# Attention and MLP on one core: the order of q and x transposes in SP's queue

## The chip, the cores and the metric

The kernel runs on one core of one Trainium2 chip. The metric is device time in microseconds for one execution. Five engines run side by side, each with a queue of its own: TensorE (PE in the profile, its weight loads PEld), VectorE (DVE), ScalarE (ACT), GpSimd (POOL) and SyncE (SP). SP computes nothing here; it issues DMAs.

## The reference

Four sequences of 768 positions, 8 heads of 64. Attention sees four sink positions and a window of 128; the result goes through a layer norm and a two-layer MLP with a residual:

```python
keep = is_sink | in_window            # 4 sinks, 0 <= rel < 128
scores = np.where(keep, scale * q @ k.T, -1e9)
a = softmax(scores)
x = (a @ v) as (B, S, 512)
xn = (x - mu) / sqrt(var + 1e-6) * g_ln
out = x + relu(xn @ w_ch1) @ w_ch2    # 512 -> 2048 -> 512
```

## The kernel before, in words

The rows are cut into 24 tiles `t` of 128 rows, and into 12 chunks `c` of two tiles. Six tiles make a sequence. For each chunk the kernel loads k, q and v, transposes k and q (`kT`, `qT`), and computes scores, exponentials, masks and the product with v for each tile. `normalise` then takes mean and variance of the result `x`, writes the centred tile `xc` (L866) and transposes it into `xnt`. `mlp(c)` reads `xnt` of both tiles of its chunk: first layer (L1027, 64 matmuls for a chunk), relu on ScalarE (L1037), second layer (L1056), and the sum with the residual `ot` (L1064), which SP stores (L1068).

Where transposes are done changes along the way. k and q of chunks below `by_dma` = 4, and x of chunks below `x_by_dma` = 3, are transposed by TensorE and copied out of PSUM. From there on they are DMA transposes that SP issues, all from one line, L571 (`dma_t`), told apart by their tiles: `kT<-nat`, `qT<-nat` and `xnt<-xc`, two of each for a chunk.

The work of tiles from the fourth chunk on is in `block(t)`: on TensorE it holds the product with v of tile t-1 (L934, L941, L950) and the scores of tile t (L961, and L969 for the sinks on even t). So tile 7 gets its product with v, and with it `xc`, in block 8; and q of chunk c is first read by block 2c. The MLP of chunk c-2 runs between block 2c-1 and block 2c: `xnt` of tile 2c-3 must be there by then. Second-layer matmuls (L1056) of older chunks fill the time between blocks.

The order on every engine is made by a planner written out in the kernel. Each piece of work is a `P.op` with a name, the engines that it may run on, a priority, its buffers and its predecessors. `Plan.run` walks through them with estimated durations, including estimates of when a DMA lands, and gives each engine a fixed order; the program is then emitted in that order. A predecessor given with `after=` counts for these estimates, and so for the order. What the engines wait for on the chip comes from the buffers that the emitted instructions read and write.

Loads of k, q and v are issued by GpSimd (L671 for k and q, L595 for v). `gate(c)` holds the loads of a chunk in the planner behind the GpSimd part of the layer norm of an earlier tile (`rs_op`, L871 and L872): for c > 5 that of tile 2c-4, for c = 5 that of tile 5. On SP, each k transpose then follows its load, and so does each q transpose; the x transpose follows `xc`, and the store follows `ot`. At the start of a sequence SP also issues two small copies `vs_s<-vs` (L540).

Of the kernel before, what the change touches and what calls it, by code (L numbers as in the profile page):

```python
# [196 lines left out]
def pe(us):  # L197
    return {"PE": (us, us + Plan.PE_DRAIN)}
# [12 lines left out]
def fix(occ, extra=0.09):  # L211
# [8 lines left out]
HW_X = (1.0, -0.2, 0.6)  # L220
# [10 lines left out]
PAR = dict(strict=400.0, win=0.4, tr=-8.0, sc=-5.0, sc1=-2.0, av=2.0, blk=-8.0, step=6.0, trx=9.0, by_dma=4, x_by_dma=3,  # L231
           w1p=(1.6, 2.6, 2.7, 2.8), pm=3, w2p=(4.5, 4.51, 4.52, 4.53), apart=2, vs0=(2.0, 13.0), by_tile=1, vp=(0.0, 0.1, 2.0, 2.1, 4.55, 4.56), ld1=0.05)
# [135 lines left out]
def kernel(  # L368
# [32 lines left out]
    P = Plan()  # L401
# [104 lines left out]
    def negs(e):  # L506
# [17 lines left out]
         writes=[Bc["gt"]], dma=HW_T)  # L524
    for h in range(H):
# [3 lines left out]
            reads=[Bc["vc"]], writes=[Bc["vcd"]], nb=3.5 + 0.55 * h)  # L529
    for b in range(B):  # L530
# [4 lines left out]
            reads=[Bc["vcd"], Bc["vc"], Bc["sel4" if b else "sel"]], writes=[Bvs[b]], nb=PAR["vs0"][1] if b == 0 else 40.0 * b)  # L535
# [11 lines left out]
    for c in range(4):  # L547
        P.op(f"w2ld{c}", {"POOL": (0.75, 0.8)}, PAR["w2p"][c], lambda e, c=c: G.dma_start(
            w2[c], moe_w_ch2[512 * c:512 * (c + 1), :].rearrange("(t p) n -> p t n", p=128)),
            writes=[Bw2[c]], dma=SW_W)  # L550

    def at(c, step):
        return 16.0 * c - 8.0 + PAR[step]
# [3 lines left out]
    xnt_b = [Buf(f"xnt{c}", "xnt") for c in range(NC)]  # L557
# [4 lines left out]
    def early(t):  # L562
        return 0.5 + 0.8 * t

    rs_op = {}

    def gate(c):
        return [rs_op[2 * c - (4 if c > 5 else 5)]] if PAR["by_dma"] < c < NC else []

    def dma_t(dst, src):  # L570
        nc.sync.dma_start_transpose(out=dst, in_=src)  # L571
# [26 lines left out]
    def evict(name, prio, n, src, dst, reads, writes, fp=False):  # L598
        du = {"ACT": act(n), "DVE": dve(n) if fp else dve(n, 0.52)}
        P.op(name, du, prio, lambda e: (nc.scalar.copy if e == "ACT" else V.tensor_copy)(dst(), src()),  # L600
             reads=reads, writes=writes)

    def chunk(c):
        b, R = c // RC, c % RC
        d = at(c, "tr") if c >= 2 else early(2 * c)
        ld = d - 14.0 if c >= RC else 4.0
        if c < 2:
            kT_b[c], qT_b[c] = Buf(f"kT{c}", "kT"), Buf(f"qT{c}", "qT")
            if c == 0:
                nats = [Buf("kf", "natf"), Buf("qf", "natf")]  # L610
                for hh in range(2):
                    hs = slice(4 * hh, 4 * hh + 4)
                    for i, (x, T) in enumerate(((k, kT_b[c]), (q, qT_b[c]))):
                        nm, src, part = "kq"[i], nats[i], Buf(f"{'kq'[i]}l{hh}")
# [4 lines left out]
                        nat, pt, done = Buf(f"{nm}c{hh}", "natc"), Buf(f"pt{nm}{hh}", "one"), Buf(f"{nm}T0{hh}")  # L619
                        P.op(f"cast{nm}{hh}", {"DVE": dve(512), "ACT": act(512)}, d + 0.01 * hh,  # L620
                             lambda e, nat=nat, src=src, hs=hs: (nc.scalar.copy if e == "ACT" else V.tensor_copy)(
                                 nat.t, src.t[:, hs].rearrange("p h i d -> p i h d")),
                             reads=[part], hold=[src], writes=[nat])

                        def tr(e, pt=pt, nat=nat):
                            pb = pt.t.rearrange("p (h m i) -> p h m i", h=2, i=2)
                            for hp in range(2):
                                for i in range(2):
                                    nc.tensor.matmul(pb[:, hp, :, i], lhsT=nat.t[:, i, 2 * hp:2 * hp + 2, :], rhs=ident,  # L629
                                                     start=hp + i == 0, stop=True, skip_group_check=True)  # L630
# [7 lines left out]
            for t in (2 * c, 2 * c + 1) if c else ():  # L638
                d, at_t = early(t), slice(128 * (t % 2), 128 * (t % 2) + 128)
                if c:  # L640
                    pt = Buf(f"pt{t}", "one")
                    for i, (x, T) in enumerate(((k, kT_b[c]), (q, qT_b[c]))):
                        nat = Buf(f"{'kq'[i]}n{t}", "nat")
                        ap = x[b, :, 128 * t:128 * t + 128, :].rearrange("h p d -> p h d")
                        P.op(f"{'kq'[i]}ld{t}", {"POOL": (0.87, 0.9)}, PAR["ld1"] + 0.2 * (t - 2) + 0.01 * i,
                             lambda e, nat=nat, ap=ap: G.dma_start(nat.t, ap), writes=[nat], dma=SW)

                        def tr(e, nat=nat, pt=pt, i=i):
                            pb = pt.t.bitcast(BF16)
                            for hp in range(HP):  # L650
# [3 lines left out]
                                       reads=[nat, Bc["ident"]], hold=[T], **({"rw": [pt]} if i else {"writes": [pt]}))]  # L654
# [6 lines left out]
        else:  # L661
            for nm, src, bT in (("k", k, kT_b), ("q", q, qT_b)):
                T = Buf(f"{nm}T{c}", nm + "T")
                bT[c] = T
                pt = Buf(f"pt{nm}{c}", "one")
                for i in range(2):
                    if c >= PAR["by_dma"]:
                        nat = Buf(f"{nm}n{c}{i}", "nat")
                        ap = src[b, :, 256 * R + 128 * i:256 * R + 128 * (i + 1), :].rearrange("h p d -> p h d")
                        P.op(f"{nm}ld{c}{i}", {"POOL": (0.87, 0.9)}, ld + 0.01 * i + (0.1 if nm == "q" else 0.0),  # L670
                             lambda e, nat=nat, ap=ap: G.dma_start(nat.t, ap), writes=[nat], dma=SW, after=gate(c))  # L671
                        P.op(f"tr{nm}{c}{i}", {"SP": (1.2, 1.2)}, d + 0.01 * i, lambda e, T=T, nat=nat, i=i: dma_t(
                            T.t[:, :, 128 * i:128 * i + 128], nat.t.rearrange("p h d -> p (h d)")),
                            reads=[nat], writes=[T], dma=HW_X)
                        continue
                    nat = Buf(f"{nm}n{c}{i}", "nat")
                    ap = src[b, :, 256 * R + 128 * i:256 * R + 128 * (i + 1), :].rearrange("h p d -> p h d")
                    P.op(f"{nm}ld{c}{i}", {"POOL": (0.87, 0.9)}, ld + 0.01 * i + (0.1 if nm == "q" else 0.0),
                         lambda e, nat=nat, ap=ap: G.dma_start(nat.t, ap), writes=[nat], dma=SW)

                    def tr(e, nat=nat, pt=pt, i=i):
                        pb = pt.t.bitcast(BF16)
                        for hp in range(HP):
                            nc.tensor.transpose(pb[:, 256 * hp + 128 * i:256 * hp + 128 * (i + 1)],
                                                nat.t[:, 2 * hp:2 * hp + 2, :], ident)
                    P.op(f"tr{nm}{c}{i}", pe(0.224), d + 0.01 * i, tr, reads=[nat, Bc["ident"]], hold=[T],
                         **({"rw": [pt]} if i else {"writes": [pt]}))
                if c < PAR["by_dma"]:
                    evict(f"ev{nm}{c}", d + 0.2, 1024,
                      lambda pt=pt: pt.t.bitcast(BF16).rearrange("p (h c) -> p h c", h=HP),  # L690
                      lambda T=T: T.t, [pt], [T])
# [167 lines left out]
    def normalise(c, i, d, st, x, xc):  # L859
        t = 2 * c + i  # L860
        mv = Buf(f"mv{t}")
        P.op(f"bn{t}", {"DVE": fix(0.60)}, d + 0.12, lambda e: V.bn_stats(st.t[:, 8:14], x.t),  # L862
             reads=[x], writes=[st, mv])
        P.op(f"ag{t}", {"DVE": fix(0.09)}, d + 0.13, lambda e: V.bn_aggr(st.t[:, 14:16], st.t[:, 8:14]),  # L864
             reads=[st], rw=[mv])
        P.op(f"xc{t}", {"DVE": fix(0.26)}, d + 0.14, lambda e: V.tensor_scalar(  # L866
            xc.t, x.t, st.t[:, 14:15], None, op0=ALU.subtract), reads=[x, st, mv], writes=[xc])
        rs = Buf(f"rs{t}")
        xst_b[t, "rs"] = rs
        rs_op[t] = P.op(f"rs{t}", {"POOL": (0.83, 0.88)}, d + 5, lambda e: (  # L870
            G.tensor_scalar(st.t[:, 17:18], st.t[:, 15:16], 1e-6, None, op0=ALU.add),  # L871
            G.tensor_tensor(st.t[:, 16:17], st.t[:, 17:18], mhalf, op=ALU.pow)),  # L872
            reads=[st, mv, Bc["mhalf"]], writes=[rs])
        pt = Buf(f"ptx{t}", "one")

        def tr(e):
            pb = pt.t.bitcast(BF16)
            for j in range(NDM):
                nc.tensor.transpose(pb[:, 128 * j:128 * (j + 1)], xc.t[:, 128 * j:128 * (j + 1)], ident)  # L879
        if c >= PAR["x_by_dma"]:  # L880
            P.op(f"trx{t}", {"SP": (1.2, 1.2)}, d + 0.5, lambda e: dma_t(xnt_b[c].t[:, :, 128 * i:128 * i + 128], xc.t),
                 reads=[xc], writes=[xnt_b[c]], dma=HW_X)
            return
        d = at(c, "trx") + 1.0 * i if c >= 2 else d + 0.2
        P.op(f"trx{t}", pe(0.224), d, tr, reads=[xc, Bc["ident"]], writes=[pt],
             hold=[xnt_b[c]])
        src = lambda: pt.t.bitcast(BF16)[:, 0:512].rearrange("p (j c) -> p j c", j=NDM)
        dst = lambda: xnt_b[c].t[:, :, 128 * i:128 * i + 128]
        P.op(f"evx{t}", {"DVE": dve(512), "ACT": (1.2, 1.3)}, d + 0.1, lambda e: (
            V.tensor_tensor(dst(), src(), gt.unsqueeze(2).to_broadcast([128, NDM, 128]), op=ALU.mult) if e == "DVE" else  # L890
            [nc.scalar.mul(dst()[:, j], src()[:, j], gt[:, j:j + 1]) for j in range(NDM)]),
            reads=[pt, Bc["gt"]], writes=[xnt_b[c], xnt_t[t]])
# [191 lines left out]
    for c in range(NC):  # L1084
        mlp(c)
        if c == PAR["x_by_dma"] - 1:
            for s in range(4):
                for j in range(NDM):
                    P.op(f"w1g{s}{j}", {"DVE": fix(0.26)}, 16.0 * c + 11.0 + 2 * s + 0.1 * j,
                         lambda e, s=s, j=j: V.tensor_scalar_mul(w1[s][:, j, :], w1[s][:, j, :], gt[:, j:j + 1]),  # L1090
                         reads=[Bw1[s], Bc["gt"]], writes=[Bw1g[s]], after=last_use[s])

    def guard(e):
# [8 lines left out]
         reads=[pt_f], writes=[fl_b])  # L1102
# [4 lines left out]
    t = 1.2  # L1107
    for o in order:
# [5 lines left out]
        if n > 0 and o.start - t > 0.6:  # L1114
            free = [(max([e_ for b_, e_ in banks[i].lives if b_ < t], default=0.0), i) for i in range(8)
                    if all(e_ < t or b_ > o.start + 0.3 for b_, e_ in banks[i].lives)]
            if free:
                i = min(free)[1]
                items.append((t + 0.001, -n, pairs[i // 2][:, i % 2, :] if i < 4 else ones[i - 4]))
        t = o.start + o.engs["PE"][0]  # L1120
# [49 lines left out]
```

## Time and profile before

| | |
|---|---|
| median of 3 runs | 220.84 us (219.8 to 221.86) |
| profiled execution | 220.41 us |
| its span, first to last instruction | 218.8 us |
| TensorE busy | 208.0 us, 95% |
| VectorE, GpSimd, ScalarE busy | 118.3, 116.7, 105.3 us |
| granted TensorE clock | 1.000 |
| first layer L1027, second layer L1056 | 79.3 us and 84.8 us of TensorE |
| DMA transposes on SP | 16 of kT, 16 of qT, 18 of xnt, about 1.2 us each to issue |

Busy time is the time in which an instruction of the engine ran. A wait is idle time of an engine, put down to what ended it. On SP, a line of the timeline is the time that the queue took to issue a DMA (where two are merged, with the wait between them), not the time of the transfer. The transfer's end shows only where an instruction waited for it.

### The profile page before, as it was taken

The numbers are of one execution on the slowest core, as the hardware profiler recorded it, in microseconds if no ns is written. First come the engines' busy times: TensorE is split into PE (matmuls) and PEld (weight loads), VectorE is DVE, ScalarE is ACT, GpSimd is POOL, SyncE is SP. The second block draws the span as 40 slices with busy tenths as digits, with TensorE's granted clock in tenths as the row PEclk, the third lists the DMA queues.
The fourth block names the chain that finished last, engine by engine and source line by source line (L and its number), as shares of the span: only waits on it lengthen the run. The fifth ranks groups of instructions, "written<-read, shape, count | busy, mean of one in ns | idle before, by whom it ended". The sixth has DMA issues, their size and how long they took to land.

```text
span 218.8 us, 6430 instructions
## 1 busy us (share of the span) xinstructions
PE 208.0 (95%) x2630; PEld 146.1 (67%) x2653; DVE 118.3 (54%) x324; ACT 105.3 (48%) x167; POOL 116.7 (53%) x172
## 2 busy tenths in 40 slices
PE   6989999999999799999999999999999999999993
PEld 2658885774875585784775775774875875865852
DVE  5389882786996416716625626536445445444011
ACT  3668486254562371671571671671572562530610
POOL 7988582589972872592682692782871201201000
PEclk9999999999999999999999999999999999999999
DMA  5999999999999799299599399499699202202103
GB/s 154 162 182 206 175 206 198 158 150 120 205 146 168 126 149 140 49 170 118 122 159 179 58 163 132 113 148 144 117 137 154 90 3 75 72 3 72 48 9 105
DMA packets 110229, 27.81 MB, mean 127 GB/s; under 512 B 100464, under 2 KB 107248, under 8 KB 110192
## 3 DMA queue, kind: packets, MB, share of 16 engines
q0 software_dynamic: 76112, 13.18, 88.6%
q1 hardware_dynamic: 33024, 13.61, 33.3%
q10 hardware_dynamic: 1056, 0.52, 0.9%
q8 instruction: 23, 0.38, 0.8%
q14 instruction: 14, 0.11, 0.2%
HBM read 27.43 MB, written 6.29 MB: 154 GB/s over the span
## 4 chain that ended last, share of the span: by engine, by line
PE 87%; DVE 6%; DMA 2%; issue 2%; ACT 1%; SPq 0%; DVEq 0%
PE one L1056 36%; PE one L1027 35%; PE pair L961 3%; DMA xnt<-xc 2%; PE one L934 2%; PE pair L1126 2%; PE one L941 2%; DVE st L862 1%; DVE x L854 1%; PE one L950 1%; DVE xnt L890 1%; PE one L969 1%; PE pair L734 1%; PE one L629 1%; PE one L1020 1%
## 5 line engine op out<-in xcount | busy, mean ns | idle before, releaser
L1056 PE MATMUL one<-w,h 128*128 128x512 bf16 (+1 forms) x377 | 84.8, 370 | 2.2 <-issue 1.4
L1027 PE MATMUL one<-xnt,w 128*128 128x256 bf16 x704 | 79.3, 273 | 1.6 <-DMA xnt<-xc 1.6
L1037 ACT ACTIVATE h<-one 128x512 bf16<-128x512 f32 x95 | 56.6, 598 | 49.7 <-PE one L1027 46.4
L1027 PEld LDWEIGHTS <-w 128*128 128x128 bf16 x704 | 68.6, 98 | 12.4 <-DMA xnt<-xc 2.0
L1056 PEld LDWEIGHTS <-h 128*128 128x128 bf16 x400 | 37.3, 98 | 39.3
L979 ACT ACTIVATE pe<-pair 128x768 bf16<-128x768 f32 x36 | 27.2, 808 | 43.6 <-PE pair L961 39.2
L871 POOL TENSOR_SCALAR st<-st 128x1 f32<-128x1 f32 x24 | 8.7, 362 | 66.3 <-DVE st L864 65.7
L595 POOL DMA_DIRECT2D vn<-in_v_dram x59 | 38.7, 696 | 7.7 <-DMA w<-in_moe_w_ch_dram 3.3
L1002 DVE RECIPROCAL rec<-one 128x4 f32<-128x4 f32 x36 | 6.4, 177 | 59.6 <-PE one L950 48.1
L1064 DVE SCALAR_TENSOR_TENSOR ot<-one,st,x 128x512 f32<-128x512 f32 (+1 forms) x25 | 18.2, 728 | 13.1 <-PE one L1056 8.6
L872 POOL TENSOR_TENSOR st<-st,mhalf 128x1 f32<-128x1 f32 x24 | 16.6, 691 | 2.0
L862 DVE BATCH_NORM_STATS2 st<-x 128x6 f32<-128x512 bf16 x24 | 16.7, 695 | 0.8
L1004 DVE TENSOR_TENSOR x<-one,rec 128x256 bf16<-128x256 f32 x36 | 15.3, 425 | 1.2
L671 POOL DMA_DIRECT2D nat<-in_k_dram x16 | 15.1, 947 | 0.4 <-PE one L879 0.4
L671 POOL DMA_DIRECT2D nat<-in_q_dram x16 | 14.1, 897 | 0.0
L984 DVE TENSOR_TENSOR pe<-pe,band 128x768 bf16<-128x768 bf16 x24 | 12.3, 552 | 0.0
L866 DVE TENSOR_SCALAR xc<-x,st 128x512 bf16<-128x512 bf16 x24 | 8.8, 365 | 1.1 <-DVE st L864 0.3
L961 PE MATMUL pair<-qT,kT 64*64 64x128 bf16 (+1 forms) x528 | 9.2, 204 | 0.0
L759 ACT ACTIVATE pe<-pair 128x1024 bf16<-128x1024 f32 (+1 forms) x8 | 7.3, 920 | 3.6 <-PE pair L713 2.1
L934 PEld LDWEIGHTS <-pe 128*128 128x128 bf16 (+1 forms) x144 | 6.2, 97 | 2.9 <-issue 1.3
L1020 PE MATMUL one<-xnt,w 128*128 128x128 bf16 x128 | 7.8, 219 | 0.0
L961 PEld LDWEIGHTS <-kT 64*64 64x64 bf16 x528 | 7.2, 108 | 0.4 <-issue 0.4
(109 smaller groups left out, 171.8 us busy)
## 6 DMA issues: line engine op xcount, KB each, us to landing
out_dram<-ot SPq DMA_DIRECT2D x23, 256.0 KB
w<-in_moe_w_ch_dram POOLq DMA_DIRECT2D x8, 512.0 KB, 12.2
nat<-in_k_dram POOLq DMA_DIRECT2D x22, 128.0 KB, 4.9
nat<-in_q_dram POOLq DMA_DIRECT2D x22, 128.0 KB, 5.2
vn<-in_v_dram POOLq DMA_DIRECT2D x44, 32.0 KB, 5.2
vn<-in_v_dram POOLq DMA_DIRECT2D x15, 64.0 KB, 4.8
vn<-in_v_dram POOLq DMA_DIRECT2D x6, 128.0 KB, 6.5
natf<-in_q_dram ACTq DMA_DIRECT2D x2, 256.0 KB
```

The lines of the kernel that those rows point to most:

```text
L595: P.op(f"vld{t}_{i}", {"POOL": (0.8, 0.85)}, prio + 0.001 * i, lambda e, p0=p0, n=n, hs=hs, src=src: G.dma_start(m.t[p0:p0 + n, hs, 0:64], ...
L671: lambda e, nat=nat, ap=ap: G.dma_start(nat.t, ap), writes=[nat], dma=SW, after=gate(c))
L862: P.op(f"bn{t}", {"DVE": fix(0.60)}, d + 0.12, lambda e: V.bn_stats(st.t[:, 8:14], x.t), reads=[x], writes=[st, mv])
L872: G.tensor_tensor(st.t[:, 16:17], st.t[:, 17:18], mhalf, op=ALU.pow)),
L961: nc.tensor.matmul(pps[u].t[64 * g:64 * g + 64, h2, col + c0:col + c0 + n], lhsT=kt.t[rs, hp, k0:k0 + 64], rhs=qT.t[rs, hp, q0:q0 + n], st ...
L979: nc.scalar.activation(pes[j].t.rearrange("p a b -> p (a b)")[:, 0:768].rearrange("p (a b) -> p a b", a=2), pps[j].t[:, :, 0:384], AF.Exp, ...
L984: V.tensor_mul(at_s, at_s, band[j] if r > 1 else edge[r][j].unsqueeze(1).to_broadcast([128, 4, 192]))
L1004: P.op(f"x{t - 1}{u}", {"DVE": dve(256)}, d + 0.051 + 0.002 * u, lambda e, u=u, rc=rc, pv=pv: V.tensor_tensor(x.t[:, 256 * u:256 * u + 256 ...
L1027: nc.tensor.matmul(ph.t[:, 256 * s:256 * s + 256], lhsT=w1[ht // 4][:, j, 128 * (ht % 4):128 * (ht % 4 + 1)], rhs=xnt.t[:, j, :], start=j ...
L1037: nc.scalar.activation(hb.t, ph.t, AF.Relu)
L1056: nc.tensor.matmul(pc.t[:, 0:wd], lhsT=(h1[2 * s + i].t[:, 128 * ii:128 * ii + 128] if by_tile else h1[ht // 2].t[:, 256 * (ht % 2) + 128 ...
L1064: V.scalar_tensor_tensor(ot.t[:, sl], in0=pc.t[:, 0:wd], scalar=st.t[:, 16:17], in1=x.t[:, sl], op0=ALU.mult, op1=ALU.add),
```

## The change

For chunks c > 4, each of the two q transposes gets the x transpose of tile 2c-3 as a predecessor in the planner. That tile is three in front of the chunk's first tile, 2c. To have it at hand, `normalise` keeps the op of each x transpose in `trx_op`. No instruction is added or taken away, and k transposes, loads and stores keep their predecessors.

```diff
-    rs_op = {}
+    rs_op, trx_op = {}, {}
...
                         P.op(f"tr{nm}{c}{i}", {"SP": (1.2, 1.2)}, d + 0.01 * i, lambda e, T=T, nat=nat, i=i: dma_t(
                             T.t[:, :, 128 * i:128 * i + 128], nat.t.rearrange("p h d -> p (h d)")),
-                            reads=[nat], writes=[T], dma=HW_X)
+                            reads=[nat], writes=[T], dma=HW_X, after=[trx_op[2 * c - 3]] if c > PAR["by_dma"] and nm == "q" else [])
...
-            P.op(f"trx{t}", {"SP": (1.2, 1.2)}, d + 0.5, lambda e: dma_t(xnt_b[c].t[:, :, 128 * i:128 * i + 128], xc.t),
+            trx_op[t] = P.op(f"trx{t}", {"SP": (1.2, 1.2)}, d + 0.5, lambda e: dma_t(xnt_b[c].t[:, :, 128 * i:128 * i + 128], xc.t),
                  reads=[xc], writes=[xnt_b[c]], dma=HW_X)
```

## The prediction

> **What bounds the kernel now.** I read the page first: busy times, the chain that ended last, then the waits, the timeline of SP, and the stretches around each x transpose.
>
> The page says that TensorE carries the time. The first two lines are busy time, share of the span and instructions; the last is the chain by engine.
>
> ```profile
> span 218.8 us, 6430 instructions
> PE 208.0 (95%) x2630; PEld 146.1 (67%) x2653; DVE 118.3 (54%) x324; ACT 105.3 (48%) x167; POOL 116.7 (53%) x172
> ...
> PE 87%; DVE 6%; DMA 2%; issue 2%; ACT 1%; SPq 0%; DVEq 0%
> ```
>
> So a change on SP, which computes nothing, is worth only what TensorE waits for SP's transfers: look at the 2% of DMA. The waits of TensorE alone (us in total, times, longest) name it: one wait for a transposed x.
>
> ```profile
> PE pair L1126 <- DVE one_e L464: 1.8, 1, 1.8
> PE one L1027 <- DMA xnt<-xc: 1.6, 1, 1.6
> PE one L1056 <- issue: 1.4, 9, 0.2
> ```
>
> The first of these is in the startup, the third is nine gaps of at most 0.2 us that name no transfer. The middle one is the only place after the startup where TensorE stands. By stretches (length, then busy us and count of each engine) it lies in the stretch that ends at 73.2 us; afterwards every chunk looks alike:
>
> ```profile
> 63.00:73.20 10.20, 8.44 (x131) 4.33 (x121) 8.09 (x23) 3.32 (x6) 4.27 (x9) 1.00 1.61 128
> 73.20:89.60 16.40, 16.19 (x224) 11.55 (x227) 7.04 (x20) 8.09 (x13) 8.86 (x13) 1.00 1.76 135
> 89.60:105.50 15.90, 15.69 (x196) 10.77 (x196) 7.99 (x21) 7.97 (x13) 9.78 (x14) 1.00 1.72 134
> ...
> 154.00:170.20 16.20, 15.99 (x224) 11.33 (x225) 7.96 (x20) 8.08 (x13) 9.52 (x14) 1.00 1.47 133
> ```
>
> From 73.2 us on a chunk leaves TensorE 16.40 - 16.19 = 0.21 us idle (15.90 - 15.69 and 16.20 - 15.99 are the same 0.21), and none of that names a DMA. The granted clock is 1.00 in each of these stretches, so no clock is in play.
>
> **The one wait, step by step.** The timeline of that place, SP and VectorE and TensorE together (start, length, engine, operation, count, idle before):
>
> ```profile
> 59.60 5.61 SPq L571 DMA_TRANSPOSE kT<-nat  x2
> ...
> 65.38 2.72 SPq L571 DMA_TRANSPOSE qT<-nat  x2
> ...
> 65.69 0.35 DVE L866 TENSOR_SCALAR xc<-x,st 128x512 bf16<-128x512 bf16 x1
> ...
> 68.20 1.21 SPq L571 DMA_TRANSPOSE xnt<-xc  x1
> ...
> 69.97 1.67 PE L1056 MATMUL one<-w,h 128*128 128x512 bf16 x7 [0.16 <-issue]
> ...
> 73.19 3.01 PE L1027 MATMUL one<-xnt,w 128*128 128x256 bf16 x26 [1.55 <-DMA xnt<-xc]
> ```
>
> The centred tile 7 (`xc`) is ready at 65.69 + 0.35 = 66.04. SP has issued both k transposes of chunk 5 by 59.60 + 5.61 = 65.21, but then issues both q transposes (2.72 us), and only at 68.20 the x transpose of tile 7. TensorE has finished its other work at 69.97 + 1.67 = 71.64, and starts the MLP of chunk 3 at 73.19: 1.55 us idle. The chain of waits shows the transfer as 4.95 us from its issue:
>
> ```profile
> 67.14 0.96 SPq L571
> 68.20 4.95 DMA xnt<-xc
> 73.19 7.16 PE one L1027 x64
> ```
>
> **The change, part by part.**
>
> It adds and removes no instruction. It gives each q transpose of chunk c >= 5 the x transpose of tile 2c-3 as a predecessor in the hand-written planner. The planner only orders the queues, so on the chip SP does not wait until that transpose has landed; it has it ahead of it in its queue. The seven pairs are q of chunks 5 to 11 with tiles 7, 9, ..., 19. In the trace the q pair stands ahead of its x in all seven (80.04 ahead of 83.62, 97.92 ahead of 101.70, and so on), so all seven turn round.
>
> *What is gained on chunk 5.* The x transpose of tile 7 needs `xc` (66.04) and an idle SP (65.21), so it starts near 66.1 and not at 68.20: 2.1 us earlier. How long it takes from there is not shown, so I bound it. Shortest: for tile 15 the same issue at 134.72 was answered by an MLP that began at 138.09 without a wait, so at most 3.37 us. The row itself: 4.95 us, behind two q transposes and beside loads. Longest: the slowest transfer of the trace in this place, the first q load of chunk 5, issued at 58.13, for which GpSimd was held until 67.14: 9.0 us. These give landings at 69.5, 71.1 and 75.1. TensorE needs it at 71.64. I take 4.95, the row of this very transfer: 0.6 us in time, the wait of 1.55 us is gone. At 3.37 the answer is the same; at 9.0 the wait is 3.4 us, which is 1.9 us more than now.
>
> [...]
>
> *What is gained on chunks 6 to 11.* The x transposes start earlier here too where SP had q ahead of a ready `xc`: tile 11 at 99.83 in place of 101.70, tile 15 at 132.07 in place of 134.72. Their MLPs wait for nothing now, so this is worth nothing. The cover is TensorE's own queue: the MLP of chunk 5 cannot start before 105.5 because the matmuls ahead of it end there. If the cover were gone, 1 to 2.6 us would be the worth of each.
>
> *What is moved back.* The q pairs. Counted with everything that they are moved past: the x transpose (1.2 us), and most likely the store behind it, since the planner holds the q pair until it believes x has landed. Chunk 5: x 66.1 to 67.3; the store waits for `ot` (VectorE L1064, 67.22 + 0.75 = 67.97) and takes 0.53; q from about 68.5 to 71.0, still ahead of the next x at 72.05. The second q starts at 69.8; with 4.95 us it lands at 74.8. Its user, the scores of block 10, now start at 80.79, or 79.24 with the gain: 4.5 us to spare. Chunk 6 is the tightest, because two copies `vs_s` (L540, 86.39 to 87.50) also come first: the second q starts at about 88.9, lands at 93.9, and block 12 reads it at 97.03: 3.1 us to spare (both ends move alike with the gain). Chunk 9: store after `ot` at 134.42, second q at about 136.3, landing 141.3, read at about 145.5: 4.2 us. So I cost the move at nothing; what hides it is the time that TensorE still spends on L1027 and L1056 before the block that reads q. Ends for this cost: 0 at 4.95 us; at 9.0 us chunk 6 would be 9.0 - 8.1 = 0.9 us late, chunks 5 (9.4 to spare from issue) and 9 (9.2) not. Nothing else is behind the waiting q on SP but the x of the next tile, needed a chunk later, and stores.
>
> *What the freed TensorE meets next.* The MLP of chunk 3 starts at 71.64. Its first hidden tile needs a PSUM bank; two were freed by the x products (VectorE, done at 70.7). From the second chunk on the same pattern (blocks, seven L1056, then L1027) runs without a gap, for example at 89.4, so I see no next wait. The loads of chunk 6 hang on the statistics of tile 8 (GpSimd at 71.72), which do not move, and their transposes end at 82.6 for a user at 95.5.
>
> *Sum.* -1.55 (wait) + 0 (other x) + 0 (q) = -1.55 us. The profiled execution took 220.41 us, 218.8 of it the span and 1.6 around it: 218.86 after. It lies 0.43 under the median of the three runs, 220.84; against that median the forecast is **219.3 us**, 0.7% faster.
>
> **Rivals.**
>
> *A, the wait stays, wholly or in part.* The x transpose starts 2.1 us earlier, but lands when the loads let it. For it: in the slice 66 to 67 us the DMA share is 3.16, against 0.52 at 71 to 72, so it is moved into the crowd. Against it: seven later pairs work beside the same loads without a wait. If half of it stays: 220.84 - 0.8 = 220.0; if all stays, or if the queue keeps its order after all and so the change does nothing, 220.8.
>
> *B, slower: transposes under the loads.* One mechanism: near 66 us the transposes take as long as the q load did, 9.0 us. It takes away the gain from 5.6 us (71.64 - 66.05) on, and costs from 7.1 us (73.15 - 66.05) on. Then tile 7 lands at 75.1, +1.9 us, and q of chunk 6 is 0.9 us late: 220.84 + 2.8 = 223.6. [...] Against it: 4.95 us is what the same transfer took with the q pair ahead of it and the loads still running, and from 67 to 68 us the share has fallen to 2.14.
>
> [...]
>
> *C, more than the profile's wait.* Runs spread from 219.8 to 221.86, and the profiled one is a fast one. If slower runs wait longer for tile 7, as much as 1.55 + 1.0, the median falls by 2.6: 218.3. For it: the wait depends on loads, the likeliest thing to vary. Against it: nothing in one trace shows it.
>
> **How the numbers follow.** The forecast has 0.62, A 0.14, B 0.12, C 0.12. A change under 1% (2.2 us) is about what a measurement of this kernel can't tell from none. The forecast's own range, with half a microsecond or a little more of run spread, is 218.5 to 220.2. C's 218.3 and a fast draw of it set the low end at 217.7; A lies inside, and half of B beside a slow draw sets the high end at 221.6. Faster by over 1% is C and an eighth of the forecast (0.12 + 0.08 = 0.20); slower by over 1% is B and a little for slow draws (0.13); the rest, 0.67, is within 1%.
>
> **What would show it.** In the profile after: on SP, kT x2, xnt, (store), qT x2, in seven chunks; the x transpose of tile 7 near 66.1; the wait of L1027 for `xnt` gone from TensorE's list; the stretch of the MLP of chunk 3 starting near 71.6; later chunks at 0.21 us of idle each; the span near 217.3. It is wrong if L1027 still waits for `xnt` (A, B), if L961 waits for `qT` (B), or if a new gap of TensorE follows at 71 to 90 us.

## The result, and the profile after

The changed kernel took 219.27 us (median of 20 executions, 217.97 to 220.41), the kernel before 220.68 us (20 executions, 219.01 to 223.23). The ratio is 0.994, 95% interval 0.9919 to 0.9961: 1.3 us less (0.9 to 1.8). Ratios leave out executions more than 1.5% above the fastest of their kernel, medians keep them, so a ratio can differ from that of two medians. The four queues other than SP hold the same instructions in the same order; on SP the x transpose now stands ahead of the q pair in all seven chunks. The forecast of 219.3 us holds. The reason given for it holds only in part, as the experiments show.

The page after, first lines, against 218.8 us and the same busy times before:

```profile
span 217.8 us, 6429 instructions
PE 208.0 (95%) x2630; PEld 146.3 (67%) x2653; DVE 118.2 (54%) x324; ACT 105.4 (48%) x167; POOL 116.6 (54%) x172
```

TensorE does the same work in less span. Its waits (us in total, times, longest) have lost the one for `xnt`, and nothing has come in its place (the longest two; L1126 and the rest of the list are startup):

```profile
PE pair L1126 <- DVE one_e L464: 1.8, 1, 1.8
PE one L1056 <- issue: 1.4, 9, 0.2
```

The nine gaps of L1056 stand only in this profile and in that of before, whose pages count 2630 matmuls. The twelve other profiles count 2653 and list no such gap, so these are most likely matmuls that are missing from the record, and not waits.

The same place in the timeline after:

```profile
60.33 3.91 SPq L571 DMA_TRANSPOSE kT<-nat  x2
...
65.72 0.35 DVE L866 TENSOR_SCALAR xc<-x,st 128x512 bf16<-128x512 bf16 x1
...
66.10 1.19 SPq L571 DMA_TRANSPOSE xnt<-xc  x1
...
68.28 0.34 SPq L1068 DMA_DIRECT2D out_dram<-ot  x1
68.78 2.83 SPq L571 DMA_TRANSPOSE qT<-nat  x2
...
71.76 4.42 PE L1027 MATMUL one<-xnt,w 128*128 128x256 bf16 x39
```

The x transpose goes out at 66.10, as soon as `xc` is there, and no longer at 68.20. The store follows, then q. L1027 follows L1056 without a gap.

For exact bookkeeping I split each span at two points of the chain of waits: the start of the MLP of chunk 2 and that of chunk 11. Between them lies everything that the change can touch.

| | start | middle | end | span |
|---|---|---|---|---|
| before | 55.39 | 145.69 | 17.72 | 218.8 |
| after | 55.68 | 144.03 | 18.09 | 217.8 |

The middle lost 1.66 us. Start and end, which the change doesn't touch, were 0.29 and 0.37 us longer in this execution. That is the span's 1.0; the forecast for the span was 217.3 us.

### The profile page after: what moved, and what is told of

It reads as the page before. It is cut to its first block, busy times and chain, and to the rows that moved or that the text cites. A ratio compares the mean times of both kernels' runs of the same rounds, so it can differ in the third digit from the quotient of the medians.

```text
span 217.8 us, 6429 instructions
## 1 busy us (share of the span) xinstructions
PE 208.0 (95%) x2630; PEld 146.3 (67%) x2653; DVE 118.2 (54%) x324; ACT 105.4 (48%) x167; POOL 116.6 (54%) x172
## 4 chain that ended last, share of the span: by engine, by line
PE 89%; DVE 6%; issue 2%; ACT 1%; DVEq 0%
PE one L1056 38%; PE one L1027 35%; PE pair L961 3%; PE one L934 2%; PE pair L1126 2%; PE one L941 2%; DVE st L862 1%; DVE x L854 1%; PE one L950 1%; DVE xnt L890 1%; PE one L629 1%; PE one L969 1%; PE pair L734 1%; DVE xc L866 1%; PE one L1020 1%
## 5 line engine op out<-in xcount | busy, mean ns | idle before, releaser
L1056 PE MATMUL one<-w,h 128*128 128x512 bf16 (+1 forms) x377 | 84.8, 370 | 2.2 <-issue 1.4
L1027 PE MATMUL one<-xnt,w 128*128 128x256 bf16 x704 | 79.3, 273 | 0.0
L1027 PEld LDWEIGHTS <-w 128*128 128x128 bf16 x704 | 68.7, 98 | 10.7 <-issue 0.5
L1056 PEld LDWEIGHTS <-h 128*128 128x128 bf16 x400 | 37.3, 98 | 39.3
```

The costliest lines, as they stand in the source:

```text
L1027: nc.tensor.matmul(ph.t[:, 256 * s:256 * s + 256], lhsT=w1[ht // 4][:, j, 128 * (ht % 4):128 * (ht % 4 + 1)], rhs=xnt.t[:, j, :], start=j ...
L1056: nc.tensor.matmul(pc.t[:, 0:wd], lhsT=(h1[2 * s + i].t[:, 128 * ii:128 * ii + 128] if by_tile else h1[ht // 2].t[:, 256 * (ht % 2) + 128 ...
```

## The experiments

Three groups of four kernels; the kernels of a group ran on one chip, beside executions of the kernel before (medians 219.41, 220.64 and 220.42 us). Each group had another chip, so a time is compared only inside its group. "q first" is the order of before, "x first" that of the change.

### Half the change each, first time

`e1_only5`: the predecessor for chunk 5 alone. `e2_not5`: for chunks 6 to 11 alone. (The end of one line is shown.)

```diff
-after=[trx_op[2 * c - 3]] if c > PAR["by_dma"] and nm == "q" else []
+after=[trx_op[2 * c - 3]] if c == 5 and nm == "q" else []      # e1
+after=[trx_op[2 * c - 3]] if c > 5 and nm == "q" else []       # e2
```

> The predecessor is given to the q pair of chunk 5 alone; chunks 6 to 11 keep q ahead of x. Theory (the whole gain is the one wait of TensorE for tile 7): as the changed kernel, about 1.3 to 1.55 us under the kernel before, no wait of L1027 for xnt. Rival 1 (all seven pairs bring a little each, the wait moves elsewhere): a seventh to a half of the gain, 0.2 to 0.7 us. Rival 2 (the gain is something else, such as less DMA crowding later): none of it without chunks 6 to 11.

> The predecessor is given to the q pairs of chunks 6 to 11, chunk 5 keeps q ahead of x. Theory: as the kernel before within run spread (ratio 1.000, at most 0.3% off), and the wait of L1027 for the xnt of tile 7 is there again, 1 to 2 us. Rivals 1 and 2: half or all of the 1.3 us gain stays.

Measured: e1 219.67 us, ratio 1.0014 (0.9984 to 1.0045); e2 218.86 us, ratio 0.9998 (0.9962 to 1.0034). e1 missed its expectation: no gain. But this group held no execution of the whole change, so it does not show that there was a gain to divide on this chip. e2's ratio is as expected, but not for the reason given, because its profile has q first in chunk 5 and still no wait for tile 7:

```profile
64.07 2.51 SPq L571 DMA_TRANSPOSE qT<-nat  x2
...
66.68 1.21 SPq L571 DMA_TRANSPOSE xnt<-xc  x1
```

Here the q pair went out from 64.07 without a wait between its two issues and x at 66.68, 1.5 us earlier than in the profile of before, and the MLP started at 71.63 without a wait. So the wait that the prediction was built on belongs to some executions, not to the kernel.

### When x lands

`e3_probe_before`, `e4_probe_after`: GpSimd copies one column after each odd tile's x transpose.

```diff
+            if i:
+                P.op(f"prb{t}", {"POOL": (0.3, 0.35)}, d + 4.0, lambda e: G.tensor_copy(prb, xnt_b[c].t[:, 0, 255:256]),
+                     reads=[xnt_b[c]], writes=[Buf(f"prb{t}")])
```

> The kernel before with one more instruction per chunk from chunk 3 on: GpSimd, idle there, copies one column of xnt after the x transpose of each odd tile, so that its wait shows when the transfer lands. Theory: tile 7 lands 4.9 to 5 us after its issue, just before the MLP of chunk 3 starts, and tiles 9 to 19 land 3.0 to 4.5 us after issue, ahead of their MLPs. Rival (TensorE waits for something else that ends at the same time): the probe ends clearly ahead of the MLP of chunk 3.

> The changed kernel with the same probes. If the landing moves just with the issue, tile 7 lands 4.95 us after it, near 71.0. If in SP's queue the data of the q pair stood ahead of it, the time from issue to landing falls to 3.0 to 3.5 us here and falls by about 1 us for later tiles too. If the loads of GpSimd set it (rival B), it rises over 5.6 us, and L1027 waits.

Measured: 219.7 and 219.14 us, one execution each. e3 missed its expectation for tile 7: 4.27 us in place of 4.9 to 5, and no wait of the MLP. e4 gave 4.25 us there, which is none of its three cases (4.95, 3.0 to 3.5, over 5.6). The probe's start, after its idle time on the DMA, is the landing. Tiles 7 and 9, q first and then x first:

```profile
70.46 0.19 POOL L885 COPY prb<-xnt 128x1 bf16<-128x1 bf16 x1 [3.66 <-DMA xnt<-xc]
86.77 0.19 POOL L885 COPY prb<-xnt 128x1 bf16<-128x1 bf16 x1 [4.47 <-DMA xnt<-xc]
```

```profile
69.75 0.19 POOL L885 COPY prb<-xnt 128x1 bf16<-128x1 bf16 x1 [2.07 <-DMA xnt<-xc]
86.14 0.19 POOL L885 COPY prb<-xnt 128x1 bf16<-128x1 bf16 x1 [3.78 <-DMA xnt<-xc]
```

With the issues from SP's timeline, all tiles (us):

| tile | 7 | 9 | 11 | 13 | 15 | 17 | 19 |
|---|---|---|---|---|---|---|---|
| issue, q first | 66.19 | 82.92 | 99.39 | 115.53 | 131.57 | 148.15 | 163.63 |
| to landing | 4.27 | 3.85 | 3.09 | 4.01 | 3.19 | 2.97 | 4.16 |
| issue, x first | 65.50 | 81.48 | 97.73 | 113.62 | 129.90 | 146.15 | 162.04 |
| to landing | 4.25 | 4.66 | 4.76 | 2.56 | 4.05 | 4.47 | 3.06 |

x is issued 0.7 to 2.0 us earlier throughout. The time from issue to landing is no shorter without the q pair ahead of it (means 3.65 and 3.97), so what moves the landing is the issue, and part of that is eaten: tile 11 was issued 1.7 us earlier and landed at the same time. Tiles 21 and 23, with no loads beside them, took 2.5 us. Neither profile waits for `xnt`.

### Late q loads, in both orders

`e6_lateq_before`, `e7_lateq_after`: the q loads of chunk 5 go behind its v loads in GpSimd's queue. Besides, the changed kernel (`e5_after_again`) and the kernel before (`e8_before_again`) as they are.

```diff
-    items = [(o.start, o.seq, o) for o in order]
+    v_last = max(o.start for o in order if o.name.startswith("vld11_"))
+    items = [(v_last + 0.001 if o.name in ("qld50", "qld51") else o.start, o.seq, o) for o in order]
```

> The changed kernel again, beside other executions of the kernel before. Theory now (the wait for tile 7 is there only in executions where the k and q loads of chunk 5 land late): the median moves by the mean of a wait that is sometimes 0 and sometimes 1 to 3 us, so between 0 and 1.5 us less than before, and the changed kernel spreads less upward. Rival (a fixed gain of 1.5 us in every execution): ratio 0.993 once more.

> The kernel before, with the two q loads of chunk 5 moved behind the five v loads of that chunk in GpSimd's queue, so that they are issued about 3.4 us later; nothing else moves. Theory (q in front of x hands the lateness of the q loads to the MLP of chunk 3): the x transpose of tile 7 is issued near 69.5 to 70.5, lands 4.3 us later, L1027 waits 2 to 3 us for xnt, and the time grows by as much. Rival (the wait comes from slow transfers and not from the queue's order): a wait of under 0.5 us.

> The same late q loads in the changed kernel. Theory: the x transpose of tile 7 is issued at 66 as before, no wait of L1027 for xnt, no wait of L961 for qT, and the time is that of the changed kernel, 2 to 3 us under the kernel before with late q loads. Rival (the wait comes from slow transfers): the same wait in both orders. Rival B (a late q costs at the scores): L961 waits for qT at block 10.

> The kernel before once more with a profile. Theory now: where the second q transpose of chunk 5 is issued by 66 us, the x transpose of tile 7 goes out by 67.3 and there is no wait; where it is issued later, L1027 waits for what that is over. A wait of 1.5 us beside an x transpose issued at 66.7 would speak against it.

Measured: e5 219.26 us, ratio 0.9954 (0.9926 to 0.9982). e6 221.74, ratio 1.0045 (1.0005 to 1.0086). e7 219.19, ratio 0.9936 (0.9906 to 0.9966). e8 218.26, one execution. The late loads cost the old order about 1 us (0.1 to 1.9) and the new one nothing. e5's ratio alone does not leave out its rival, a fixed gain with 0.993. Its executions spread as its theory has it: before they run from 219.15 to 224.03 us, after from 218.4 to 220.83, so the upper end moved by 3.2 us and the lower by 0.75. The 20 executions each of the result moved by 2.8 and 1.0. Timeline of e6 and then of e7:

```profile
61.08 1.84 POOL L671 DMA_DIRECT2D nat<-in_q_dram  x2
...
67.04 2.50 SPq L571 DMA_TRANSPOSE qT<-nat  x2
...
69.64 1.93 SPq L571 DMA_TRANSPOSE xnt<-xc  x1
...
72.86 3.34 PE L1027 MATMUL one<-xnt,w 128*128 128x256 bf16 x29 [1.67 <-DMA xnt<-xc]
```

```profile
65.83 1.19 SPq L571 DMA_TRANSPOSE xnt<-xc  x1
...
68.17 3.50 SPq L571 DMA_TRANSPOSE qT<-nat  x2
...
71.14 5.08 PE L1027 MATMUL one<-xnt,w 128*128 128x256 bf16 x45
```

With q first, lateness of a q load reaches x, and through x TensorE (1.67 us, somewhat under the 2 to 3 expected, since x then took 3.2 us and not 4.3). With x first it ends in q's own slack. e6 also shows what the prediction denied: L1027 waited 0.36 us at 105.52 and 0.17 us at 122.09, at the MLPs of chunks 5 and 6, which this edit doesn't touch (its list of waits comes first below, then that of e8). e8, the kernel before, has its wait there too: 0.20 us for `xnt` at the MLP of chunk 5, none at chunk 3, with the q pair issued from 64.61 and x at 67.23, as the expectation had it.

```profile
PE one L1027 <- DMA xnt<-xc: 2.2, 3, 1.7
```

```profile
PE one L1027 <- DMA xnt<-xc: 0.2, 1, 0.2
```

The kept traces also hold the updates that DMAs made to semaphores; the last update of a transfer is read as its landing here. Landings read so lie within 0.15 us of every probe's start and every end of a wait shown here (x of tile 7 in the kernel before: 73.14, and L1027 began at 73.19). In the six profiles with q first in chunk 5 they tie the wait to the load (us):

| | e3 | e2 | e11 | e8 | before | e6 |
|---|---|---|---|---|---|---|
| second q load landed | 64.42 | 65.14 | 65.56 | 65.71 | 66.85 | 67.53 |
| x of tile 7 issued | 66.19 | 66.68 | 66.92 | 67.23 | 68.20 | 69.64 |
| L1027 waited | 0 | 0 | 0 | 0 | 1.55 | 1.67 |

The later the load, the later x, and the last two make TensorE wait. In e7, x first, the load landed at 68.13, later than in any of these, and x was issued at 65.83.

### Half the change each, second time

`e9_after` is the changed kernel; `e10_only5_again` and `e11_not5_again` are e1 and e2 once more.

> The changed kernel, the reference point for the two halves of the change on the same chip: between 0.3 and 1.5 us under the kernel before, by how often the loads of chunk 5 are late here. No wait for xnt.

> The q pair of chunk 5 alone behind its x. Theory (the wait for tile 7 is the main part, the x of tiles 11 and 13 are within 0.3 us of waiting): most of what the whole change gains here, with at most small waits of L1027, up to 0.5 us, at the MLPs of chunks 5 and 6. Rival (the other six pairs carry it): none of the gain.

> The q pairs of chunks 6 to 11 behind their x, chunk 5 as before. Theory: at most a third of the gain; in the slower executions L1027 waits for tile 7. Rival: all of the gain.

Measured: e9 219.06 us, ratio 0.9957 (0.9921 to 0.9993). e10 220.42, ratio 1.001 (0.9966 to 1.0053). e11 218.64, ratio 0.9967 (0.993 to 1.0004). e10's theory fell: the pair of chunk 5 alone brings nothing that can be measured, in either group, and e10's interval, from 0.9966 up, leaves out e9's 0.9957, though the two intervals overlap. e11 gains about as much as e9, though its interval touches 1, and the same kernel as e2 showed 0.9998 in its group. So these ratios don't divide the gain among the chunks. e10's profile shows where its time went:

```profile
129.70 3.94 SPq L571 DMA_TRANSPOSE qT<-nat  x2
130.57 0.35 DVE L866 TENSOR_SCALAR xc<-x,st 128x512 bf16<-128x512 bf16 x1
133.73 1.22 SPq L571 DMA_TRANSPOSE xnt<-xc  x1
...
138.17 1.05 PE L1027 MATMUL one<-xnt,w 128*128 128x256 bf16 x8 [1.23 <-DMA xnt<-xc]
```

This is tile 15 and the MLP of chunk 7. `xc` is ready at 130.92, but the q pair holds SP for 3.94 us, 1.4 more than two issues take, and x goes out 2.8 us late. It is the picture that the prediction found at tile 7, four chunks later; there the k pair ahead of q had been held up as well (5.61 us). In e9, x first, at the same place:

```profile
129.47 0.35 DVE L866 TENSOR_SCALAR xc<-x,st 128x512 bf16<-128x512 bf16 x1
129.85 1.19 SPq L571 DMA_TRANSPOSE xnt<-xc  x1
132.20 0.35 SPq L1068 DMA_DIRECT2D out_dram<-ot  x1
132.65 3.49 SPq L571 DMA_TRANSPOSE qT<-nat  x2
...
135.68 1.58 PE L1027 MATMUL one<-xnt,w 128*128 128x256 bf16 x13
```

Over all profiles of these kernels (the one below left out), the seven MLPs with q first were seen 42 times, and six of them show a wait for `xnt`: at chunk 3 (1.55, and 1.67 with the loads made late), chunk 5 (0.36, 0.20), chunk 6 (0.17), chunk 7 (1.23). With x first they were seen 49 times, and none shows a wait (the views leave out gaps under 0.15 us). The landings say how near the others were. This is the time from the landing of the odd tile's x to the start of its MLP, lowest to highest (us):

| MLP of chunk | 3 | 4 | 5 | 6 | 7 | 8 | 9 |
|---|---|---|---|---|---|---|---|
| q first | 0.05-0.79 | 0.06-2.13 | 0.13-0.72 | 0.14-2.49 | 0.04-1.15 | 0.34-1.49 | 0.14-0.67 |
| x first | 0.48-2.22 | 0.71-1.88 | 0.13-0.78 | 2.68-3.41 | 1.22-2.24 | 1.01-1.68 | 1.01-3.23 |

Where TensorE did wait, the MLP started 0.04 to 0.14 us after the landing, so a value of that size means that nothing was in hand. The median is 0.46 us with q first and 1.37 with x first. At chunk 5 the change leaves little: in its first profile and in e5 the value is 0.14 and 0.13, and TensorE has a gap of 0.03 and 0.06 us there. The middle stretch tells the same:

| | order | middle, us |
|---|---|---|
| before; again (e8); late q (e6) | q first | 145.69; 144.20; 146.54 |
| only chunk 5 (e1; e10) | mostly q first | 143.87; 145.53 |
| not chunk 5 (e2; e11) | mostly x first | 143.85; 143.85 |
| after; again (e5; e9); late q (e7) | x first | 144.03; 144.07; 143.85; 143.86 |

With x first it stays within 0.22 us of 143.85. With q first it reaches this value at best. (The probes: 144.07 with q first, 143.85 with x first.) In the five profiles with q first in six or seven chunks and no load moved (before, e10, e8, e1, e3), the waits come to 1.55, 1.23, 0.20, 0 and 0, 0.6 us in the mean, and the ratios of the whole change to 0.9 to 1.3 us. Five profiles are too few to say whether the wait for `xnt` is the whole gain.

### q pushed further back

`e12_q_last`: the q pair behind the next x transpose and store too.

```diff
-    items = [(o.start, o.seq, o) for o in order]
+    at_op = {o.name: o.start for o in order}
+    behind = {f"trq{c}{i}": at_op[f"st{2 * c - 5}0"] + 0.001 for c in range(5, NC) for i in range(2)}
+    items = [(behind.get(o.name, o.start), o.seq, o) for o in order]
```

> The changed kernel with each q pair moved further back on SP, behind the next x transpose (tile 2c-2) and the store after it; all other queues as they are. The second q is then issued 3.7 to 3.9 us ahead of the scores that read it. If q takes the 4.95 us of the prediction's row, L961 waits about 1.1 us in each of seven chunks, 7 to 8 us in all. If it takes what the probes showed for x, 2.5 to 4.8 us, the waits are 0 to 0.9 us each, 1 to 4 us in all. If q has far more slack than thought, nothing.

Measured: 251.58 us, ratio 1.1455 (1.1361 to 1.155). All three expectations were far too small. The waits of TensorE:

```profile
PE one L969 <- DMA qT<-nat: 13.2, 6, 3.6
PE pair L961 <- DMA qT<-nat: 7.3, 6, 2.2
```

20.5 us of waits, in six chunks. The chain gives the second q transpose of each, from issue to use (start, length; the other three took 7.26, 7.64 and 6.71):

```profile
75.27 8.72 DMA qT<-nat
...
161.51 6.53 DMA qT<-nat
181.49 8.65 DMA qT<-nat
```

Each was issued while GpSimd was issuing the next chunk's k and q loads (72.6 to 76.2 around the first). Chunk 11 has no next chunk; its second q was issued at 204.60, landed 2.5 us later by its semaphore, and was not waited for. So 6.5 to 8.7 us beside the loads, 2.5 without. The span is 249.6, 32 us over e9's 217.6. Beside 20.5 us of waits, L1056 was busy for 97.8 us and not 84.8: after the waits of five of the six chunks TensorE ran for a while at a lower granted clock, seen here around the first (length, busy times, clock in the third column from the right):

```profile
81.00:84.00 3.00, 0.00 (x0) 0.00 (x0) 1.47 (x4) 0.82 (x2) 1.68 (x4) 0.71 3.11 93
...
86.00:88.00 2.00, 2.00 (x6) 0.76 (x5) 0.00 (x0) 0.00 (x0) 0.00 (x0) 0.50 0.81 94
...
90.00:92.00 2.00, 2.00 (x14) 0.94 (x13) 1.33 (x4) 0.00 (x0) 0.00 (x0) 1.00 0.00 0
```

## Why the prediction was right, and where it was not

*The mechanism held.* SP's queue has the order turned round in all seven chunks, and q is issued without waiting for x's landing (tile 7 in e4: q from 68.09, x landed at 69.75). The x transpose of tile 7 was forecast at 66.1 and issued at 66.10; q was forecast from about 68.5 and came at 68.78; the wait of L1027 is gone and no new one follows. e6 and e7 show the cause by itself: the same late loads cost 1.67 us at tile 7 in one order and nothing in the other.

*The size held, from a sum with a wrong term.* -1.55 us was forecast, -1.3 measured (-1.8 to -0.9). That the two lie so close is in good part luck: 1.55 was the longest of the waits in the five profiles with q first (in six or seven chunks) and no load moved, and two of these had none. The step "What is gained on chunks 6 to 11 ... is worth nothing" failed. It took TensorE's own queue for a cover, and called the wait at 71.64 "the only place after the startup where TensorE stands". That was one execution. In others the wait was at chunks 5, 6 or 7, and the part of the change for chunk 5 alone gained nothing in 12 executions of each of two groups. So the -1.55 of one chunk stood in for a wait that wanders over several. The profile held the hint: tile 15's MLP started 3.37 us after the issue of its x. The prediction used that as an upper bound for a transfer and still put 4.95 us on the same kind of transfer at tile 7. By the landings, the MLPs with q first had 0.46 us in hand at the median, and x took 2.5 to 4.95 us. A cover smaller than the spread of what it hides is no cover. The predicted variation of the wait with the loads (rival C) was right in its ground, but C put it at tile 7 and made the gain larger, which the runs don't show.

*x's transfer.* 4.95 us was taken. The probes gave 2.6 to 4.8 beside loads in both orders, the semaphores of all these profiles 2.4 to 5.6. The second case of e4's expectation, a shorter transfer once the q pair is no longer ahead of it, was not seen: the mean went from 3.65 to 3.97 us (by the semaphores from 3.62 in 42 cases to 4.04 in 49). So the landing gained less than the issue, 1.2 us of 1.6 in the mean of the probes' seven tiles; what took the rest is not shown.

*q's slack.* "I cost the move at nothing" was right, with more to spare than was said. The scores that need the second q are L969. In the changed kernel that q of chunk 6 was forecast to land at 93.9; by its semaphore it landed at 91.1, and L969 read it at 95.87: 4.7 us in hand where 3.1 were forecast. q took less than the 4.95 us put on it, 2.4 to 4.8 with x first against 2.4 to 7.3 with q first, and, e12 aside, no profile with x first waits for `qT`. e12 shows the end of that slack: 6.5 to 8.7 us where the issue falls beside the next chunk's loads. The 9.0 us named for rival B, as the time of the first q load, was misread. SP issued the transpose of that load at 65.38, at most 7.3 us after its issue; what GpSimd was held for until 67.14 was the second load, issued at 58.99 and landed at 66.85. B's place for so long a transfer (tile 7 near 66 us) was wrong too.

*Open.* What makes k and q loads land a microsecond or two later in some executions was not found (the second q load of chunk 5 landed at 64.42 to 66.85 us in the five profiles with q first there and no load moved), and the shares of the seven chunks in the gain can't be told from these runs. Nor is it shown that the waits for `xnt` make up the whole of it.

## What to carry to other kernels

Where a queue issues in the program's order, as SP's did here (in e10 x was ready at 130.92 and went out at 133.73, after the q pair), a request whose input is ready should not stand behind one that still waits for a load and is needed later: here that order cost nothing in a good execution and 1.2 to 1.7 us in another. A wait in one profile tells where lateness surfaced that time; before the same pattern elsewhere is called covered, compare its margin with the spread of the transfer, and take several profiles. Moving the other request back was free here only to a point: where its transfer met the next batch of loads, it took 6.5 to 8.7 us (e12) and TensorE waited.

## What the hardware showed that was not expected

A DMA transpose of 128x512 bf16 within SBUF took 2.4 to 2.5 us from issue to landing with no loads beside it and 2.4 to 5.6 us in the usual place of x. The same transpose of q took 5.2 us in the mean ahead of x, 3.2 behind it, and 6.5 to 8.7 us for the second of a pair issued beside the next chunk's loads.

In e12, TensorE's granted clock fell to 0.50 around its waits: it was 0.50 from 84 to 88 us, so that 24 matmuls L1056 took 7.68 us in place of 5.35. The first drop came inside the wait of 3.59 us, which began at 80.4: the clock was 1.00 from 81 to 82 us and 0.64 from 82 to 83. In four more chunks the clock fell to 0.50 around a pair of waits with 0.4 to 0.5 us of scores between them, and the longer wait of the pair was 2.16, 1.70, 1.65 and 2.25 us. In the sixth, waits of 0.66 and 1.80 us left it at 1.00. The pairs 0.81 and 1.65 (a drop) and 0.66 and 1.80 (none) add up to the same 2.46 us, so the length of the waits alone did not decide it here; what did is not shown. After the single wait of 1.55 us in the kernel before the granted clock stayed at 1.00.
